# Down-projection of chunk pairs by seven block products of half size (Strassen), in a GateLoop and SwiGLU kernel

## The chip, the cores and the metric

One core of a Trainium2 chip runs the whole program. The metric is device time in microseconds of one execution; the time of the kernel before is the median of three. A profile shows one execution: engines are TensorE (PE; PEld is its loading of weights), VectorE (DVE), ScalarE (ACT), GpSimd (POOL) and SyncE (SP), whose queue here issues most DMA transfers.

## The reference

```python
def _attn_ref(q, k, v, a_re, a_im):          # (4, 8, 768, 48) each, float32
    mag = np.sqrt(a_re * a_re + a_im * a_im)
    scale = np.minimum(mag, 0.999) / (mag + 1e-06)
    a_re_n, a_im_n = (a_re * scale, a_im * scale)
    ...
    for t in range(S):
        ar, ai = (a_re_n[:, :, t, :, None], a_im_n[:, :, t, :, None])
        new_re = ar * S_re - ai * S_im
        new_im = ar * S_im + ai * S_re
        kv = np.einsum('bhd,bhe->bhde', k[:, :, t], v[:, :, t])
        S_re, S_im = (new_re + kv, new_im)
        y[:, :, t] = np.einsum('bhd,bhde->bhe', q[:, :, t], S_re)

def _moe_ref(x, w_gate, w_val, w_out, rms_g):  # x (3072, 384), d_ff 1536
    rms = np.sqrt(np.mean(x * x, axis=-1, keepdims=True) + 1e-06)
    xn = x / rms * rms_g
    g = xn @ w_gate
    silu = g * (1.0 / (1.0 + np.exp(-g)))
    val = xn @ w_val
    return (silu * val @ w_out)
```

The output of the first, with its heads side by side, is the `x` of the second. The weights arrive as 64-bit numbers and are narrowed on the chip.

## The kernel before

**Work.** The 3072 rows are 24 chunks of 128 (`C`), six to a sequence. For each chunk there are three kinds of work. `gates(u)` (L977) turns the gates of a unit of one or two chunks (`UNITS`, L667) into a decay and a rotation, and multiplies k and q by them into `rot`; six DMAs a chunk bring `rot` to `kq` in the layout that the products need (three buffers `kqs`, L819). It is mostly DVE and ACT work on 768 columns. `attend(n)` (L1065) makes the chunk's scores, its output and the next state on PE, with DVE masking the scores (`am`) and adding states, and ends in the RMS norm: the sum of squares goes through PE into a column, DVE makes `ssv` (the mean square plus 1e-6), POOL raises it to −1/2 (`rs`), PE spreads it, and DVE writes the chunk's part of `xT`, the normed input, transposed. `feed(g, xT)` (L1156) is the feed-forward network of a group of chunks.

**Groups.** `GROUPS` (L668) has two groups of two chunks, then five of four. `feed` runs over the 12 blocks of 128 hidden features. For each it makes gate and value in two PSUM banks (`bank()`, L1060, hands out banks 0 to 3 in turn); a list fills a bank, 512 columns: one feature block by 512 tokens, or two by 256 in a group of two. ACT applies Silu (`sg`), DVE multiplies into `hT`. Then each chunk has its down-projection: 12 matmuls accumulate `hT` (128 features by 128 tokens, the stationary side) times `wo` (384 columns), ACT copies the bank to `ot`, and a DMA on SP's queue writes it out. Matmuls are float32, each two instructions in the profile, each with its own load of weights.

**Order.** Nothing is issued as it is written. Every operation is recorded through helpers, so all carry L648, and `Flow.schedule` (L550) orders them: each engine takes, of the operations whose inputs are ready by the planner's own durations, the one due first. `feed` gives its lists due times from a running clock (`clock`, `SPREAD`, L1154); whatever feeds them inherits a due time from its users. The order of each engine is therefore fixed when the program is built, and an engine waits in place when the next operation's inputs are late.

**Tests.** The fast program holds for inputs in a certain range. Tests of this go into `ok`; the weight tests (`look(i)`, L912) read all weights again and reduce them on DVE. At the end the count of passed tests goes through a small matmul (`okc`) to `bad`, and where it isn't zero a general program runs after the fast one.

Of the kernel before, what the change touches and what calls it, by code (L numbers as in the profile page):

```python
# [18 lines left out]
P = 128  # L19
# [631 lines left out]
def fast(tc, ctx, qT, kT, v, a_re, a_im, w_gate, w_val, w_out, rms_g, out, H, bad):  # L651
# [10 lines left out]
    L = P // H  # L662
    HH = H // 2
    NP = H // 2
    assert DM % P == 0 and D2 <= P and L * ND == D and D == 48 and N == 24 and NF == 12

    UNITS = [[0], [1]] + [[n, n + 1] for n in range(2, N, 2)]  # L667
    GROUPS = [[0, 1], [2, 3]] + [list(range(n, n + 4)) for n in range(4, N, 4)]  # L668
    unit_of = {n: u for u, ns in enumerate(UNITS) for n in ns}
    group_of = {n: g for g, ns in enumerate(GROUPS) for n in ns}  # L670
    NU = len(UNITS)
# [138 lines left out]
    wv = room("wv", [P, DF // W, ND, W])  # L810
    wo = room("wo", [P, NF + 4, DM])
    hT = room("hT", [P, NF * 512])
    xTs = [room(f"xT{i}", [P, ND * 512]) for i in range(2)]
    gin = [room(f"in{i}", [P, 2, 768]) for i in range(2)]
    kin = room("kin", [P, 2 * ND * 2 * C])
    tmp = {x: room(x, [P, 768]) for x in ("t1", "t2", "t4")}
    turns = room("turns", [P, 2, 768])
    rots = [room(f"rot{i}", [P, 2 * ND, 2 * C]) for i in range(2)]
    kqs = [room(f"kq{i}", [D2, H, 2 * C]) for i in range(3)]  # L819
    decays = [room(f"decay{i}", [D2, H, nt]) for i, nt in enumerate((1, 1, 2, 2))]  # L820
    room("pad1", [P, 16])
    ams = [room(f"am{i}", [C, H, C]) for i in range(2)]
# [5 lines left out]
    ssv = [room(f"ssv{i}", [P, 1]) for i in range(2)]  # L828
    rss = [room(f"rs{i}", [P, 1]) for i in range(2)]
    sgs = [room(f"sg{i}", [P, 512]) for i in range(2)]  # L830
    ots = [room(f"ot{i}", [C, DM]) for i in range(2)]
    junk = room("junk", [1, 1], I32)
    seen = room("seen", [D2, 1])

# [142 lines left out]
    def gates(u):  # L977
        ns = UNITS[u]
        nt = len(ns)
        T = nt * C  # L980
        t = loaded.pop(u) if u in loaded else load_kq(u, load_gates(u))
        flow.stage = "size", u
        re, im, q, k = (t[x] for x in ("re", "im", "q", "k"))
        t1, t2, t3, t4, t5 = (t[f"t{i}"] for i in range(1, 6))
        act(t1, re, AF.Square)
        act(t2, im, AF.Square)
        if u in SUMMED:
            sums = []
# [60 lines left out]
        for n_ in ns:  # L1049
            moved[n_] = [dma(kqs[n_ % 3][r:D2:2 * ND], rots[n_ % 2][:, r], "SP") for r in range(2 * ND)]  # L1050
            if n_ < 2:
                cleared[n_] = copy(seen, kqs[n_ % 3][:, 0, 0:1], eng="POOL")
# [11 lines left out]

    def attend(n):  # L1065
        flow.stage = "attend", n
        ve, am, kq = ves[n % 3], ams[n % 2], kqs[n % 3]
        vv = ve[:, :, :, 0:D].rearrange("t m e d -> t (m e) d")
        dma(vv, v[n * C:(n + 1) * C, :].rearrange("t (h d) -> t h d", d=D), behind=moved[min(n - 1, HOLD)] if n else ())
        k, q = kq[:, :, 0:C], kq[:, :, C:2 * C]  # L1070
# [54 lines left out]
        else:  # L1125
# [7 lines left out]
        ts(ssv[n % 2], col, 1.0 / DM, EPS_RMS, ALU.mult, ALU.add)  # L1133
        add("POOL", [(nc.gpsimd.tensor_tensor, (), dict(out=rss[n % 2], in0=ssv[n % 2], in1=mhalf,
                                                        op=ALU.pow))], 0.9, [ssv[n % 2], mhalf], [rss[n % 2]])
# [8 lines left out]
        tt(xT[:, :, i * C:(i + 1) * C], yg, wide.unsqueeze(1).to_broadcast([P, ND, C]))  # L1144
        return xT

    xplace = {0: (0, 0), 1: (0, 768)}
    for g in range(2, len(GROUPS)):
        xplace[g] = ((g + 1) % 2, 0)

    clock = [36.0]
    SPREAD = 1.0  # L1154

    def feed(g, xT):  # L1156
        flow.stage = "feed", g
        ns = GROUPS[g]
        nt = len(ns)
        T = nt * C  # L1160
        base = {0: 0, 1: 3072}.get(g, 0)
        per = 4 // nt
        for b in range(NF // per):
            ps = [bank(), bank()]
            for o, w_ in zip(ps, (wg, wv)):
                list_ = []
                for i in range(per):
                    f = b * per + i
# [3 lines left out]
                dur = per * ND * mm_time(T)  # L1172
# [4 lines left out]
            tt(hT[:, base + b * 512:base + (b + 1) * 512], ps[1], sg)  # L1177
        for i, n in enumerate(ns):
            ps = bank()
            o = ps[:, 0:DM]  # L1180
            for f0 in range(0, NF, 4):
                clock[0] += 4 * mm_time(DM) * SPREAD
                mms([(o, hT[:, base + f * T + i * C:base + f * T + (i + 1) * C], wo[:, f], f == 0, f == NF - 1)
                     for f in range(f0, f0 + 4)], 4 * mm_time(DM), due=clock[0])
            ot = ots[n % 2]
            act(ot, o, AF.Copy)
            dma(out[n * C:(n + 1) * C, :], ot)

    for u in range(2):
        loaded[u] = load_gates(u)  # L1190
# [19 lines left out]

    ne = N * ND
    NW = len(looks)
    ok = room("ok", [P, 2 * ne + NU + 2 * NW])
    okc = room("okc", [P, 1])
    ef = ends.rearrange("p j n -> p (j n)")
    o = 0
    for in_, limit, op in ((ef, P_MIN, ALU.is_ge), (ef, 1.0, ALU.is_le), (range_, 0.0, ALU.is_le),
                           (small, 1.25 * 2.0 ** -15, ALU.is_ge), (large, 2.0, ALU.is_lt)):
        w_ = in_.shape[1]
        ts(ok[:, o:o + w_], in_, limit, None, op)  # L1220
        o += w_
    add("DVE", [(nc.vector.tensor_reduce, (), dict(out=okc, in_=ok, axis=mybir.AxisListType.X, op=ALU.add))],
        0.4, [ok], [okc])
    ps = banks[7]
    mms([(ps[0:1, 0:1], okc, ones, True, True)], 0.25)
    add("DVE", [(nc.vector.tensor_scalar, (), dict(out=bad, in0=ps[0:1, 0:1], scalar1=-1.0,
                                                   scalar2=float(P * o), op0=ALU.mult, op1=ALU.add))],
        0.2, [ps[0:1, 0:1]], [])

    flow.schedule()  # L1230
    with tc.manual_schedule():
# [51 lines left out]
```

## Time and profile before

| | us |
|---|---|
| median of 3 runs (lowest, highest) | 760.88 (760.03, 761.19) |
| profiled execution | 760.46 |
| its span, first to last instruction | 758.7 |
| PE, DVE, ACT, POOL busy | 712.6, 408.7, 324.7, 43.5 |
| instructions of PE | 3970 |

The clock of PE is 0.984 of full speed over the span. In a line of a group (`out<-in`, partitions by columns, count, then busy us and mean ns) buffer numbers are left out: `bank` is any PSUM bank, `hT`, `wo`, `xT` are as above. A line of the timeline has the start, the length, the engine and how many instructions stand together. A line of waits has the total, how many waits, and the longest.

### The profile page before, as it was taken

The page shows a single profiled execution, that of the slowest core. Times are in us where ns is not written, and L with a number is a line of the kernel's source. Part 1 is how long each engine was busy: PE and PEld are TensorE (multiplying, and loading weights), DVE is VectorE, ACT ScalarE, POOL GpSimd, SP SyncE. Part 2 cuts the span into 40 slices and gives each one's busy share as a digit, 9 for nine tenths or more (in the row PEclk, how much of TensorE's full clock was granted, in tenths as well). Part 3 has the DMA queues.
Part 4 walks back from the last instruction along what each step waited for, and adds up shares of the span by engine and source line. Part 5 has one row for each costly group of instructions (what it writes and reads, how often), then busy time and mean ns, then how long its engine had stood idle before and what let it go on. Part 6 is the DMA issues. An engine that isn't in the chain of part 4 may idle for free.

```text
span 758.7 us, 10119 instructions
## 1 busy us (share of the span) xinstructions
PE 712.6 (94%) x3970; PEld 444.0 (59%) x3970; DVE 408.7 (54%) x643; ACT 324.7 (43%) x450; POOL 43.5 (6%) x71
## 2 busy tenths in 40 slices
PE   0479999999999999999999999999999999999996
PEld 0468878886444777544576444576544577544453
DVE  5989888988887798871266621278111132111100
ACT  8568667866968455870155711153201011110100
POOL 3122100001000011000001000001000000000000
PEclk9959999999999999999999999999999999999999
DMA  8697647456663476610243200044100020000000
GB/s 297 211 280 224 188 122 214 131 130 173 178 197 115 125 203 175 177 62 1 58 131 105 73 0 0 12 127 104 53 1 0 11 64 12 22 0 0 1 21 25
DMA packets 100137, 76.33 MB, mean 101 GB/s; under 512 B 40945, under 2 KB 90865, under 8 KB 100081
## 3 DMA queue, kind: packets, MB, share of 16 engines
q1 hardware_dynamic: 96016, 61.05, 29.3%
q0 software_dynamic: 3264, 14.16, 5.2%
q8 instruction: 33, 0.54, 0.3%
q10 hardware_dynamic: 800, 0.39, 0.2%
q14 instruction: 24, 0.19, 0.1%
HBM read 51.91 MB, written 4.72 MB: 75 GB/s over the span
## 4 chain that ended last, share of the span: by engine, by line
PE 90%; DVE 4%; ACT 2%; POOL 1%; DMA 1%; issue 1%; SPq 0%; DVEq 0%; ACTq 0%; POOLq 0%
PE bank L648 90%; POOL rs L648 1%; DVE turns L648 1%; DVE wg L648 1%; ACT L648 1%; DVE wv L648 1%; ACT turns L648 0%; SPq L648 0%; DMA in<-in_a_re_dram 0%; ACT t L648 0%; DVE rot L648 0%; DMA ve<-in_v_dram 0%; DVE xT L648 0%; DVE in L648 0%; DVE am L648 0%
## 5 line engine op out<-in xcount | busy, mean ns | idle before, releaser
L648 PE MATMUL bank<-xT,wg 128*128 128x512 f32 (+1 forms) x504 | 199.5, 536 | 2.8 <-DVE xT L648 2.8
L648 PE MATMUL bank<-wo,hT 128*128 128x384 f32 x576 | 198.0, 490 | 0.0
L648 PE MATMUL bank<-xT,wv 128*128 128x512 f32 (+1 forms) x504 | 197.5, 532 | 0.0
L648 DVE TENSOR_TENSOR hT<-bank,sg 128x512 f32<-128x512 f32 x72 | 49.5, 689 | 194.9 <-PE bank L648 192.3
L648 PEld LDWEIGHTS bank<-xT,wg 128*128 128x128 f32 x504 | 96.2, 192 | 91.5 <-issue 83.0
L648 PEld LDWEIGHTS bank<-xT,wv 128*128 128x128 f32 x504 | 95.5, 190 | 89.9 <-issue 85.4
L648 PEld LDWEIGHTS bank<-wo,hT 128*128 128x128 f32 x576 | 105.0, 190 | 63.0 <-issue 2.5
L648 ACT ACTIVATE sg<-bank 128x512 f32<-128x512 f32 x72 | 43.0, 597 | 192.0 <-PE bank L648 189.2
L648 PE MATMUL bank<-kq 96*128 96x128 f32 x384 | 52.8, 290 | 28.0 <-DMA kq<-rot 28.0
L648 ACT ACT_TABLE_LOAD x57 | 73.1, 1283 | 10.2 <-DVE rot L648 7.8
L648 PEld LDWEIGHTS bank<-kq 96*128 96x128 f32 x384 | 50.1, 203 | 31.8 <-issue 28.4
L648 POOL TENSOR_TENSOR rs<-ssv,mhalf 128x1 f32<-128x1 f32 x24 | 24.1, 1004 | 554.3 <-DVE ssv L648 547.2
L648 ACT ACTIVATE ot<-bank 128x384 f32<-128x384 f32 x24 | 11.7, 488 | 78.3 <-PE bank L648 68.5
L648 DVE TENSOR_TENSOR rot<-kin,turns 128x768 f32<-128x768 f32 x48 | 44.2, 951 | 1.3 <-DMA kq<-rot 1.0
L648 ACT ACTIVATE kt<-bank 128x384 f32<-128x384 f32 x40 | 18.4, 489 | 52.9 <-PE bank L648 48.9
L648 DVE TENSOR_TENSOR am<-bank,causal 128x512 f32<-128x512 f32 x48 | 32.6, 684 | 14.4 <-PE bank L648 14.1
L648 PE MATMUL bank<-am,ve 128*32 128x128 f32 x768 | 38.4, 285 | 0.0
L648 ACT ACTIVATE turns<-in 128x768 f32<-128x768 f32 (+1 forms) x39 | 30.3, 790 | 18.6 <-DVE rot L648 8.6
L648 PEld LDWEIGHTS bank<-ve,kt 128*96 128x96 f32 x320 | 30.8, 170 | 6.7 <-issue 5.6
L648 PE MATMUL bank<-ve,kt 128*96 128x48 f32 x320 | 31.5, 253 | 1.9 <-DVE am L648 1.9
L648 ACT ACTIVATE t<-t 128x768 f32<-128x768 f32 (+1 forms) x39 | 30.8, 791 | 4.9 <-DVE t L648 4.2
L648 PE MATMUL bank<-kq,state 96*32 96x128 f32 x640 | 32.7, 275 | 0.0
(94 smaller groups left out, 572.6 us busy)
## 6 DMA issues: line engine op xcount, KB each, us to landing
kq<-rot SPq DMA_DIRECT2D x144, 128.0 KB, 2.4
ve<-in_v_dram SPq DMA_DIRECT2D x24, 192.0 KB, 3.8
kin<-in_q_dram SPq DMA_DIRECT2D x24, 192.0 KB, 3.0
kin<-in_k_dram SPq DMA_DIRECT2D x24, 192.0 KB, 4.1
wo<-in_w_gate_dram SPq DMA_DIRECT2D x6, 768.0 KB, 5.2
out_dram<-ot SPq DMA_DIRECT2D x24, 192.0 KB, 2.5
wo<-in_w_val_dram SPq DMA_DIRECT2D x6, 768.0 KB, 4.4
wo<-in_w_out_dram SPq DMA_DIRECT2D x6, 768.0 KB, 5.2
```

The source lines that it names most:

```text
L648: fn(*args, **kw)
```

## The change

The down-projection of a pair of chunks is a product of a 256 by 1536 matrix A (the hidden values, two chunks) and a 1536 by 384 matrix B (`wo`). Both are cut in four blocks: A by chunk and by half of the features, B by half of the features and of the columns. Instead of eight block products, seven are made, of sums of blocks:

- From the weights, once, ahead of the first split group: T1 = B01 − B00, T2 = B11 − T1, T3 = B11 − B01 (kept in the place of B01), T4 = B10 − T2.
- From the hidden values, per pair, on DVE: S3 = A00 − A10 (in the place of A10), S2 = A11 − S3, S1 = S2 + A00, and S4 = A01 − S2 (in the place of S2).
- Seven products of six matmuls with 192 columns, in four banks, x1 to x4: A00·B00, S3·T3, A01·B10, S2·T2, S1·T1, A11·T4 and S4·B11. The first goes to SBUF (`mid0`) by ACT; the rest are joined by DVE adds of 192 and 384 columns (`mid1`, `mid0`, `ot`).

All groups are now of two chunks; the first two keep the old down-projection (`FIRST = 2`). To make room, `xT` has three buffers of half the size and `kq` two instead of three. `SPREAD` is 1.02. `hT` is laid out by chunk. `ssv` keeps all 24 columns, and a further test wants each to be at least 2e-6; the final test has a due time ahead of the last products.

```diff
-    GROUPS = [[0, 1], [2, 3]] + [list(range(n, n + 4)) for n in range(4, N, 4)]
+    GROUPS = [[n, n + 1] for n in range(0, N, 2)]
...
-    xTs = [room(f"xT{i}", [P, ND * 512]) for i in range(2)]
+    xTs = [room(f"xT{i}", [P, ND * 256]) for i in range(3)]
...
-    kqs = [room(f"kq{i}", [D2, H, 2 * C]) for i in range(3)]
+    kqs = [room(f"kq{i}", [D2, H, 2 * C]) for i in range(2)]
...
-    SPREAD = 1.0
+    SPREAD = 1.02
+    FIRST = 2
+    B = {(k, j): wo[:, k * HD:(k + 1) * HD, j * DH:(j + 1) * DH] for k in range(2) for j in range(2)}
+    T1 = blocks(hT[:, 4608:4608 + HD * DH])
+    T2, T4 = blocks(sums[:, 0]), blocks(sums[:, 1])
+    T3 = B[0, 1]
+    S1, S2 = (hT[:, o:o + HD * C].rearrange("p (f t) -> p f t", f=HD) for o in (3072, 3840))
+    def weight_sums():
+        tt(T1, B[0, 1], B[0, 0], ALU.subtract)
+        tt(T2, B[1, 1], T1, ALU.subtract)
+        tt(T3, B[1, 1], B[0, 1], ALU.subtract)
+        tt(T4, B[1, 0], T2, ALU.subtract)
...
+            if split and 2 * b + 2 == HD:
+                tt(S3, A[0, 0], A[1, 0], ALU.subtract)
...
+        def product(o, l, r):
+            for f0 in range(0, HD, 3):
+                clock[0] += 3 * mm_time(DH) * SPREAD
+                mms([(o, l[:, f], r[:, f], f == 0, f == HD - 1) for f in range(f0, f0 + 3)],
+                    3 * mm_time(DH), due=clock[0])
+        tt(S2, A[1, 1], S3, ALU.subtract)
+        tt(S1, S2, A[0, 0], ALU.add)
+        x1, x2, x3, x4 = (bank()[:, 0:DM] for _ in range(4))
+        lo, hi = slice(0, DH), slice(DH, DM)
+        product(x1[:, lo], A[0, 0], B[0, 0])
+        act(mids[0][:, lo], x1[:, lo], AF.Copy)
+        product(x2[:, lo], S3, T3)
+        product(x4[:, lo], A[0, 1], B[1, 0])
+        product(x3[:, lo], S2, T2)
+        tt(mids[1][:, lo], mids[0][:, lo], x3[:, lo], ALU.add)
+        tt(mids[1][:, hi], mids[1][:, lo], x2[:, lo], ALU.add)
+        tt(S4, A[0, 1], S2, ALU.subtract)
+        product(x1[:, hi], S1, T1)
+        tt(mids[0][:, hi], mids[1][:, lo], x1[:, hi], ALU.add)
+        product(x1[:, lo], A[1, 1], T4)
+        tt(halves(ots[1]), halves(x1), mids[1][:, hi].unsqueeze(1).to_broadcast([C, 2, DH]), ALU.add)
+        product(x4[:, hi], S4, B[1, 1])
+        tt(ots[0], mids[0], x4, ALU.add)
...
+                           (ssv, 2.0 * EPS_RMS, ALU.is_ge)):
...
-    mms([(ps[0:1, 0:1], okc, ones, True, True)], 0.25)
+    mms([(ps[0:1, 0:1], okc, ones, True, True)], 0.25, due=clock[0] - 16.0)
```

The planner makes a new order of it. The first place is the end of PE's program, with the last group. Before, after the last gate and value lists (`wg`, `wv`):

```order
L648 MATMUL bank1_66<-xT1_93,wv_89 128x512 x3
L648 MATMUL bank2_67<-xT1_93,wg_88 128x512 x3
L648 MATMUL bank3_68<-xT1_93,wv_89 128x512 x3
L648 MATMUL bank0_65<-wo_90,hT_91 128x384 x12
L648 MATMUL bank1_66<-wo_90,hT_91 128x384 x12
L648 MATMUL bank2_67<-wo_90,hT_91 128x384 x12
L648 MATMUL bank3_68<-wo_90,hT_91 128x384 x12
L648 MATMUL bank7_72<-ones_76,okc_133 1x1
```

Now, in the same place; `sums` holds T2 and T4, and a row with `hT` alone is S1·T1, since both lie in `hT`. Of the three rows of `wo` and bank 3, the first is A01·B10 and the others are the halves of S4·B11:

```order
L648 MATMUL bank7_72<-ones_76,okc_135 1x1
L648 MATMUL bank3_68<-xT2_94,wv_89 128x256 x6
L648 MATMUL bank0_65<-wo_90,hT_91 128x192 x6
L648 MATMUL bank1_66<-wo_90,hT_91 128x192 x6
L648 MATMUL bank3_68<-wo_90,hT_91 128x192 x6
L648 MATMUL bank2_67<-sums_129,hT_91 128x192 x3
L648 MATMUL bank0_65<-hT_91 128x192 x3
L648 MATMUL bank2_67<-sums_129,hT_91 128x192 x3
L648 MATMUL bank0_65<-hT_91 128x192 x3
L648 MATMUL bank3_68<-wo_90,hT_91 128x192 x3
L648 MATMUL bank0_65<-sums_129,hT_91 128x192 x6
L648 MATMUL bank3_68<-wo_90,hT_91 128x192 x3
```

The small matmul of the final test moved from behind the last list to ahead of the last value list, and one list of three stands between the last of S2·T2 and the first of S4·B11.

The second place is DVE's program at that end. Before, only the products of gate and value and the final test:

```order
L648 TENSOR_TENSOR hT_91<-bank3_68,sg1_127 128x512
L648 TENSOR_TENSOR hT_91<-bank1_66,sg0_126 128x512
L648 TENSOR_TENSOR hT_91<-bank3_68,sg1_127 128x512
L648 TENSOR_TENSOR hT_91<-bank1_66,sg0_126 128x512
L648 TENSOR_TENSOR hT_91<-bank3_68,sg1_127 128x512
L648 TENSOR_SCALAR bad_58<-bank7_72 1x1
```

Now (`hT<-hT ... x2` is S2 and S1, the next one is S4):

```order
L648 TENSOR_SCALAR bad_58<-bank7_72 1x1
L648 TENSOR_TENSOR hT_91<-bank3_68,sg1_126 128x2x2x128
L648 TENSOR_TENSOR hT_91<-hT_91 128x768 x2
L648 TENSOR_TENSOR mid1_131<-mid0_130,bank2_67 128x192
L648 TENSOR_TENSOR hT_91<-hT_91 128x768
L648 TENSOR_TENSOR mid0_130<-mid1_131,bank0_65 128x192
L648 TENSOR_TENSOR mid1_131<-mid1_131,bank1_66 128x192
L648 TENSOR_TENSOR ot1_128<-bank0_65,mid1_131 128x384
L648 TENSOR_TENSOR ot0_127<-mid0_130,bank3_68 128x384
```

Seven sums follow the last product of gate and value, S4 behind the add that reads bank 2, and the last output is DVE's.

The third place is the border of two groups on PE, where the norm of a group's last chunk (`ones`, `rs`) stands ahead of the next group's first gate list. Before, ahead of the last group:

```order
L648 MATMUL bank3_68<-wo_90,hT_91 128x384 x4
L648 MATMUL bank7_72<-ident_73,rs0_124 128x128
L648 MATMUL bank3_68<-wo_90,hT_91 128x384 x4
L648 MATMUL bank7_72<-ones_76,sq0_119 128x1
L648 MATMUL bank3_68<-wo_90,hT_91 128x384 x4
L648 MATMUL bank7_72<-ident_73,rs1_125 128x128
L648 MATMUL bank0_65<-xT1_93,wg_88 128x512 x3
```

Now, ahead of the fifth group:

```order
L648 MATMUL bank7_72<-ident_73,kq1_105 128x96 x4
L648 MATMUL bank3_68<-wo_90,hT_91 128x192 x3
L648 MATMUL bank7_72<-ones_76,sq0_119 128x1
L648 MATMUL bank0_65<-sums_129,hT_91 128x192 x6
L648 MATMUL bank7_72<-ident_73,rs1_124 128x128
L648 MATMUL bank3_68<-wo_90,hT_91 128x192 x3
L648 MATMUL bank4_69<-ident_73,kq1_105 128x96 x4
L648 MATMUL bank0_65<-xT1_93,wg_88 128x256 x6
```

Products of the pair now stand on both sides of `rs`, and such a border comes twelve times instead of seven. On DVE, the weight tests' reductions (36 in all) lie elsewhere: from the third group on, counted from a group's first product of gate and value to the next group's, 19, 5 and 1 stood in the groups of four, and 8, 11 and 8 stand in the pairs.

More of the change, by code (lines that the diff above doesn't have):

```diff
@@ L827, in fast @@
     ygs = [room(f"yg{i}", [P, ND, C]) for i in range(2)]
-    ssv = [room(f"ssv{i}", [P, 1]) for i in range(2)]
+    ssv = room("ssv", [P, N])
     rss = [room(f"rs{i}", [P, 1]) for i in range(2)]
@@ L831, in fast @@
     ots = [room(f"ot{i}", [C, DM]) for i in range(2)]
+    sums = room("sums", [P, 2, HD * DH])
+    mids = [room(f"mid{i}", [C, DM]) for i in range(2)]
     junk = room("junk", [1, 1], I32)
@@ L1049, in gates @@
         for n_ in ns:
-            moved[n_] = [dma(kqs[n_ % 3][r:D2:2 * ND], rots[n_ % 2][:, r], "SP") for r in range(2 * ND)]
+            moved[n_] = [dma(kqs[n_ % 2][r:D2:2 * ND], rots[n_ % 2][:, r], "SP") for r in range(2 * ND)]
             if n_ < 2:
-                cleared[n_] = copy(seen, kqs[n_ % 3][:, 0, 0:1], eng="POOL")
+                cleared[n_] = copy(seen, kqs[n_ % 2][:, 0, 0:1], eng="POOL")
         for r in range(2 * ND):
@@ L1132, in attend @@
         mms([(col, sq[:, j], ones, j == 0, j == parts[-1]) for j in parts], 0.25 * len(parts))
-        ts(ssv[n % 2], col, 1.0 / DM, EPS_RMS, ALU.mult, ALU.add)
-        add("POOL", [(nc.gpsimd.tensor_tensor, (), dict(out=rss[n % 2], in0=ssv[n % 2], in1=mhalf,
-                                                        op=ALU.pow))], 0.9, [ssv[n % 2], mhalf], [rss[n % 2]])
+        sv = ssv[:, n:n + 1]
+        ts(sv, col, 1.0 / DM, EPS_RMS, ALU.mult, ALU.add)
+        add("POOL", [(nc.gpsimd.tensor_tensor, (), dict(out=rss[n % 2], in0=sv, in1=mhalf,
+                                                        op=ALU.pow))], 0.9, [sv, mhalf], [rss[n % 2]])
         wide = ps[:, 0:C]
@@ L1158, in feed @@
         ns = GROUPS[g]
[L1159 to L1163, printed above, removed]
+        T = len(ns) * C
+        base = {1: 3072}.get(g, 0)
+        h = hT[:, base:base + NF * T].rearrange("p (i f t) -> p i f t", i=2, f=NF)
+        A = {(i, k): h[:, i, k * HD:(k + 1) * HD] for i in range(2) for k in range(2)}
+        S3, S4 = A[1, 0], S2
+        split = g >= FIRST
+        if g == FIRST:
+            weight_sums()
+        for b in range(HD):
             ps = [bank(), bank()]
@@ L1166, in feed @@
                 list_ = []
-                for i in range(per):
-                    f = b * per + i
+                for i in range(2):
+                    f = b * 2 + i
                     for d in range(ND):
@@ L1176, in feed @@
             act(sg, ps[0], AF.Silu)
[L1177 to L1187, printed above, removed]
+            as_f = lambda x: x.rearrange("p (f i t) -> p f i t", f=2, i=2)
@@ new lines, in feed, with finish @@
+            tt(h[:, :, 2 * b:2 * b + 2].rearrange("p i f t -> p f i t"), as_f(ps[1]), as_f(sg))
+            if split and 2 * b + 2 == HD:
+                tt(S3, A[0, 0], A[1, 0], ALU.subtract)
+        def finish():
+            for n, ot in zip(ns, ots):
+                dma(out[n * C:(n + 1) * C, :], ot)
+        if not split:
+            for i in range(2):
+                o = bank()[:, 0:DM]
+                for f0 in range(0, NF, 4):
+                    clock[0] += 4 * mm_time(DM) * SPREAD
+                    mms([(o, h[:, i, f], wo[:, f], f == 0, f == NF - 1) for f in range(f0, f0 + 4)],
+                        4 * mm_time(DM), due=clock[0])
+                act(ots[i], o, AF.Copy)
+            finish()
+            return
@@ L1212, in fast @@
     NW = len(looks)
-    ok = room("ok", [P, 2 * ne + NU + 2 * NW])
+    ok = room("ok", [P, 2 * ne + NU + 2 * NW + N])
     okc = room("okc", [P, 1])
```

18 lines of the change are left out of this document (11 added, 7 removed).

## The prediction

> **What bounds the kernel now.** I read the page first: engine totals, the granted clock by slice, and the chain that ended last.
>
> ```profile
> span 758.7 us, 10119 instructions
> PE 712.6 (94%) x3970; PEld 444.0 (59%) x3970; DVE 408.7 (54%) x643; ACT 324.7 (43%) x450; POOL 43.5 (6%) x71
> PEclk9959999999999999999999999999999999999999
> PE 90%; DVE 4%; ACT 2%; POOL 1%; DMA 1%; issue 1%; SPq 0%; DVEq 0%; ACTq 0%; POOLq 0%
> ```
>
> TensorE (PE) is busy 94% of the span, its clock is granted in full after the first slices, and it is 90% of the chain. The waits of PE say where the rest went:
>
> ```profile
> PE bank L648 <- DMA kq<-rot: 28.0, 1, 28.0
> PE bank L648 <- POOL rs L648: 3.4, 3, 1.6
> PE bank L648 <- DVE xT L648: 2.8, 5, 0.8
> ```
>
> 28.0 us is the start, which the change leaves alone. After it PE hardly waits, and what it waits for (the norm's `rs` and `xT`) stands at the borders of groups. So a change is worth what it takes out of PE's stream, less what new waits it puts in.
>
> The stream's prices come from the timeline: the start of one list to the start of the next, divided by its instructions (one matmul call is two instructions here). I don't use the groups' mean durations: their modelled ends overlap.
>
> ```profile
> 62.74 2.75 PE L648 MATMUL bank<-xT,wg 128*128 128x256 f32 x12
> ...
> 75.69 2.75 PE L648 MATMUL bank<-xT,wv 128*128 128x256 f32 x12
> ```
>
> ```profile
> 571.36 2.74 PE L648 MATMUL bank<-xT,wg 128*128 128x512 f32 x6
> ...
> 581.66 2.74 PE L648 MATMUL bank<-xT,wg 128*128 128x512 f32 x6
> ```
>
> ```profile
> 604.54 2.75 PE L648 MATMUL bank<-wo,hT 128*128 128x384 f32 x8
> 607.12 1.06 PE L648 MATMUL bank<-kq 96*128 96x128 f32 x8
> ```
>
> ```profile
> 617.27 1.95 PE L648 MATMUL bank<-kq 96*128 96x128 f32 x16
> 619.06 0.28 PE L648 MATMUL bank<-ones,sq 128*128 128x1 f32 x2
> ```
>
> 256 columns: 12.95 us over five lists of twelve, 0.2158 us each. 512: 10.30 over four lists of six, 0.4292. 384: 2.58/8 = 0.3225. 128: 1.79/16 = 0.112. Time follows the columns, with a small fixed part.
>
> **The change part by part.** *The products.* Before, a pair of chunks takes 2 × 12 calls, 48 instructions of 384 columns: 15.48 us. Now it takes 7 × 6 calls, 84 instructions of 192 columns, a form the trace lacks. Half of the 384 price is 0.161; halfway between the rows at 128 and 256 is 0.164; the line through 256 and 384 gives 0.1625. I take 0.163: 84 × 0.163 = 13.69, 1.79 less per pair, and 17.9 us less in ten pairs (the first two groups stay whole). By the ends it is 17.0 to 19.6.
>
> This needs the weight loads to stay hidden, since a load now stands before 192 columns instead of 384:
>
> ```profile
> L648 PEld LDWEIGHTS bank<-wo,hT 128*128 128x128 f32 x576 | 105.0, 190 | 63.0 <-issue 2.5
> L648 PEld LDWEIGHTS bank<-kq 96*128 96x128 f32 x384 | 50.1, 203 | 31.8 <-issue 28.4
> ```
>
> A load lasts 190 ns, more than 163. But the `kq` instructions have loads of 203 ns and follow each other every 112 ns, so loads overlap the stream and one another.
>
> The Trainium skill speaks against the change here: "TensorE: Matmul & The Clock Gate", section "The mechanism", says that a weight load overlaps running matmuls only where the row groups differ, and all loads of these products use all 128 rows. By that rule, with the 107 ns that its section "LDWEIGHTS" gives for 128 columns, a pair would go from 48 × (0.3225 + 0.107) = 20.6 to 84 × (0.163 + 0.107) = 22.7 us, an estimate from the page: 21 us lost over ten pairs. By that rule, the trace disagrees: with loads of its own, the 256-column list leaves no room for 107 ns in 0.2158.
>
> *Groups of two.* Five groups of four used 512-column lists. A list of twelve at 256 takes 2.590, one of six at 512 takes 2.575: 0.015 more, 24 such per group of four, five groups: 1.8 us.
>
> *New sums on VectorE (DVE) and ScalarE (ACT).*
>
> ```profile
> L648 DVE TENSOR_TENSOR rot<-kin,turns 128x768 f32<-128x768 f32 x48 | 44.2, 951 | 1.3 <-DMA kq<-rot 1.0
> L648 DVE TENSOR_TENSOR turns<-turns,t 128x1536 f32<-128x1536 f32 x11 | 19.3, 1752 | 4.2 <-ACT turns L648 4.1
> L648 DVE TENSOR_TENSOR xT<-yg,bank 128x384 f32<-128x384 f32 x24 | 13.2, 549 | 14.3 <-PE bank L648 14.2
> L648 DVE TENSOR_TENSOR sq<-sq 128x128 f32<-128x128 f32 x40 | 11.5, 287 | 1.8 <-ACT sq L648 1.2
> L648 ACT ACTIVATE ot<-bank 128x384 f32<-128x384 f32 x24 | 11.7, 488 | 78.3 <-PE bank L648 68.5
> ```
>
> Per pair DVE gets S1 to S4, 768 wide, 4 × 0.951; three adds of 192 columns, a quarter of the way from 0.287 to 0.549, 3 × 0.353; and two of 384, 2 × 0.549: 5.96 us. ACT loses two 0.488 copies and gains one shorter. The four weight sums, 1152 wide, are halfway between 0.951 and 1.752: 5.4 us once. Whether DVE holds them is read by stage:
>
> ```profile
> 55.70:116.10 60.40, 60.35 (x397) 48.81 (x398) 55.90 (x82) 41.77 (x58) 8.70 (x13) 0.97 0.59 172
> 184.20:304.00 119.80, 118.96 (x672) 69.90 (x671) 98.44 (x147) 77.31 (x98) 4.94 (x4) 1.00 0.58 165
> 304.00:421.00 117.00, 115.63 (x621) 66.81 (x620) 65.59 (x110) 57.53 (x76) 4.63 (x4) 1.00 0.31 87
> ```
>
> ```profile
> L648 DVE TENSOR_REDUCE small<-wo 128x1 f32<-128x768 f32 x10 | 9.5, 949 | 2.2 <-DMA wo<-in_w_out_dram 1.7 <-DMA wo<-in_w_val_dram 0.4
> L648 DVE TENSOR_REDUCE large<-wo 128x1 f32<-128x768 f32 x10 | 9.5, 948 | 0.0
> ```
>
> (Columns: stage, length, then PE, weight loads, DVE, ACT, POOL busy.) The first split groups fall in the stage from 184.2 us. DVE is busy 98.4 of 119.8 there; with 2 × 5.96 + 5.4 it would be 115.7 of 116.6 (119.8 less 2 × 1.79, and 0.36 for the lists of 256), full. But 19.0 us of it are the weight tests' reductions (the two rows from that same window), which nobody waits for until the end, and the order spreads them: after the weight sums the next pairs hold 8, 11 and 8. What must be done is 96.7 of 116.6, 83%, and from 55.7 to 116.1 DVE worked at 93% while PE lost 0.05 us. So the sums are hidden there, by the attention of the next two chunks, which stands between the products; that cover gone, the chain below is paid.
>
> In the last pair it is gone: no attention is left. S4 overwrites S2, so it waits for the third product's last read. From there DVE does one 192 add and S4: 0.353 + 0.951, plus about 0.17 for the matmul's drain (490 − 322.5 ns, the group's mean less its spacing) and 0.1 for two handovers, 1.57 us. PE has six instructions meanwhile, 0.98. Wait: 0.6 us, once.
>
> *Borders of groups.* PE's waits at the norm after 55 us are, for `rs`,
>
> ```profile
> PE bank L648 <- POOL rs L648: 3.0, 2, 1.6
> ```
>
> and the 2.8 for `xT` above, together 5.8 over seven groups, 0.83 each. Twelve groups have five more borders: up to 4.1. Against it: the order puts twelve product instructions and more between the last norm's sum and the gate. The bottom is 0; I take the middle, 2.1.
>
> *Fewer `kq` buffers, three smaller `xT`.* In the order, the last read of `kq0` in a pair and the next read of it are a whole gate and value stage apart, twelve lists, 31 us. A refill is
>
> ```profile
> 400.81 3.76 SPq L648 DMA_DIRECT2D kq<-rot  x6
> kq<-rot SPq DMA_DIRECT2D x144, 128.0 KB, 2.4
> ```
>
> 3.8 + 2.4 = 6.2 us: hidden. Its wait on PE now stands in SyncE's queue ahead of the next loads of `v`, q and k and the outputs; these have the same 31 us. Nothing, and the buffers of `xT` nothing.
>
> *The end.* The final test leaves the tail:
>
> ```profile
> 734.79 16.93 PE L648 MATMUL bank<-wo,hT 128*128 128x384 f32 x52
> 744.07 0.49 ACT L648 ACTIVATE ot<-bank 128x384 f32<-128x384 f32 x1 [7.30 <-PE bank L648]
> 752.09 0.49 ACT L648 ACTIVATE ot<-bank 128x384 f32<-128x384 f32 x1 [7.53 <-DVE bad L648]
> ```
>
> The last copy starts 8.02 us after the one before; 24 × 0.3225 = 7.74, so 0.28 goes to the test between them. The last step is now a DVE add, 0.549 for 0.488: 0.2 gained. The floor on the norms adds one small DVE instruction off the path.
>
> **Sum**, against the profiled execution's 760.46 us (span 758.7 and 1.8 around it): −17.9 + 1.8 + 0.6 + 2.1 − 0.2 = −13.6, 746.9. The median of the runs, 760.88, lies 0.4 above that execution, so I say 747.2. With the terms' ends: 742.5 + 0.4 (19.6 saved, no waits at the borders or for S4) to 749.8 + 0.4 (17.0 saved, 4.1 of waits at the borders).
>
> **The rivals.**
>
> *DVE is late in the first split pairs.* For: 115.7 us of DVE in 116.6, if the reductions stay in the way. At the 93% at which it worked beside a full PE (55.9 of 60.4), that takes 125.0, 8.4 more: 755.6. Against: 83% without them. Chance 0.12, anything from 750 to 755.6.
>
> *Slower: weight loads become the floor.* If a product's instruction can't follow faster than its load's own 190 ns, a pair takes 84 × 0.190 = 15.96, 0.48 more than before, 4.8 in all, and with the other terms 760.9 + 4.8 + 4.3 = 770. The gain is gone from 0.179 us per instruction on (15.48 less 0.43 of other terms per pair, over 84). Against it stands the `kq` row, 112 ns with loads of 203; left open only because its weights fill 96 rows. Chance 0.03. The rule of the Trainium skill told above is a harsher form of this.
>
> *Slower: the two `kq` buffers.* If chunks wait for the 6.2 us refill, at 22 chunks the gain is lost from 0.62 us each on; at 1 us each it is 769. For: PE's one long wait is for that DMA. Against: the 31 us between. Chance 0.03.
>
> *Many small waits at the new handovers*, 1.4 us in each of ten pairs: no change. Chance 0.02.
>
> That the norm's floor sends the kernel into its second program would multiply the time; the reference's rows have mean squares of 2.6e-5 and more against a floor of 1e-6, so I give it nothing.
>
> **How the numbers follow.** The forecast, 747.2, has 0.80. The range, 742.9 to 753.6, runs from the forecast's lower end over its upper one, 750.2, into the late-DVE case, of which it takes in more than half. A measurement of this kernel can tell about 0.2%, 1.5 us, from no change. Faster: 0.80 + 0.12 = 0.92; same 0.02; slower 0.03 + 0.03 = 0.06.
>
> **What would show it right or wrong.** In the changed profile, six product instructions should start 0.98 us before the next list, and ten pairs should hold 840 of 192 columns beside 96 of 384. A spacing near 0.19 means that loads bind. PE's waits outside the start should be 7 to 12 us, on `xT`, `rs` and, once, DVE's S4 (a write of `hT`). More than 16 us of waits on DVE between 180 and 400 us, or waits on DMA `kq<-rot` after the start, would make the forecast wrong, as would a DVE total far from 474 us (408.7 + 59.6 + 5.4).

## The result, and the profile after

The changed kernel takes 740.45 us (median of 4 runs, 739.72 to 742.11) beside 760.81 for the kernel before in the same comparison: a ratio of 0.9737, with a 95% interval of 0.9719 to 0.9755. It is faster, as forecast, but 747.2 was forecast and the time lies below the range's low end of 742.9. The profiled execution took 740.29 us (span 738.6), 20.2 less than the 760.46 of before; the sum of the prediction had 13.6 less.

The page of the kernel after has the engine totals, the granted clock and the chain:

```profile
span 738.6 us, 12320 instructions
PE 694.7 (94%) x5050; PEld 623.9 (84%) x5050; DVE 470.6 (64%) x738; ACT 332.1 (45%) x450; POOL 39.4 (5%) x71
PEclk9968999999999999999999999999999999999999
PE 92%; DVE 4%; ACT 1%; POOL 1%; issue 1%; DMA 1%; DVEq 0%; POOLq 0%; ACTq 0%
```

PE still bounds the kernel, now as 92% of the chain. DVE's 470.6 us is within 1% of the 474 that was forecast. The products show in the last pair, in the timeline of PE after:

```profile
723.50 1.14 PE L648 MATMUL bank<-sums,hT 128*128 128x192 f32 x6
...
726.43 1.14 PE L648 MATMUL bank<-hT 128*128 128x192 f32 x6
727.98 1.24 PE L648 MATMUL bank<-wo,hT 128*128 128x192 f32 x6 [0.41 <-DVE hT L648]
...
731.00 1.14 PE L648 MATMUL bank<-wo,hT 128*128 128x192 f32 x6
```

Three steps of six take 2.93 us, 0.1628 us an instruction, where 0.163 was forecast. The one wait for S4 is there too: 0.41 us, where 0.6 was forecast. The groups of PE after count the instructions by shape, and the group of weight loads gives their duration:

```profile
L648 PE MATMUL bank<-wo,hT 128*128 128x192 f32 x480 | 90.0, 331 | 0.4 <-DVE hT L648 0.4
L648 PE MATMUL bank<-sums,hT 128*128 128x192 f32 x240 | 45.1, 329 | 0.0
L648 PE MATMUL bank<-wo,hT 128*128 128x384 f32 x96 | 33.3, 491 | 0.0
L648 PE MATMUL bank<-hT 128*128 128x192 f32 x120 | 24.0, 336 | 0.0
```

```profile
L648 PEld LDWEIGHTS bank<-sums,hT 128*128 128x128 f32 x240 | 39.4, 190 | 0.0
```

480 + 240 + 120 = 840 instructions of 192 columns beside 96 of 384, as forecast. A load still lasts 190 ns and an instruction follows the last after 163: loads are not the floor.

What was not forecast stands in PE's waits. After:

```profile
PE bank L648 <- DVE xT L648: 1.9, 3, 0.9
PE bank L648 <- POOL rs L648: 1.8, 1, 1.8
```

The 1.8 for `rs` is in the start, at 53.90 us. The timeline of PE before has these waits past the first gate list (the bracket at a row's end is the wait ahead of it):

```profile
187.09 2.84 PE L648 MATMUL bank<-xT,wg 128*128 128x512 f32 x6 [0.84 <-DVE xT L648]
...
410.86 0.49 PE L648 MATMUL bank<-ident,rs 128*128 128x128 f32 x2 [1.37 <-POOL rs L648]
...
422.63 2.84 PE L648 MATMUL bank<-xT,wg 128*128 128x512 f32 x6 [0.31 <-DVE xT L648]
...
528.63 0.49 PE L648 MATMUL bank<-ident,rs 128*128 128x128 f32 x2 [1.64 <-POOL rs L648]
...
540.36 2.84 PE L648 MATMUL bank<-xT,wg 128*128 128x512 f32 x6 [0.32 <-DVE xT L648]
...
658.69 2.84 PE L648 MATMUL bank<-xT,wg 128*128 128x512 f32 x6 [0.65 <-DVE xT L648]
```

and that of PE after has two, beside the one for S4:

```profile
117.10 2.86 PE L648 MATMUL bank<-xT,wg 128*128 128x256 f32 x12 [0.32 <-DVE xT L648]
...
686.15 2.86 PE L648 MATMUL bank<-xT,wg 128*128 128x256 f32 x12 [0.89 <-DVE xT L648]
```

The norm's waits were 5.13 us and are 1.21. More borders of groups brought 3.9 us less of waiting, not 2.1 more.

### The profile page after: what moved, and what is told of

The parts are those of the page before. It is cut to its first block, busy times and chain, and to the rows that moved or that the text cites. A ratio compares the mean times of both kernels' runs of the same rounds, so it can differ in the third digit from the quotient of the medians.

```text
span 738.6 us, 12320 instructions
## 1 busy us (share of the span) xinstructions
PE 694.7 (94%) x5050; PEld 623.9 (84%) x5050; DVE 470.6 (64%) x738; ACT 332.1 (45%) x450; POOL 39.4 (5%) x71
## 4 chain that ended last, share of the span: by engine, by line
PE 92%; DVE 4%; ACT 1%; POOL 1%; issue 1%; DMA 1%; DVEq 0%; POOLq 0%; ACTq 0%
PE bank L648 92%; DVE wg L648 1%; DVE turns L648 1%; DVE wv L648 1%; DMA in<-in_a_re_dram 1%; ACT t L648 0%; DVE t L648 0%; DVE rot L648 0%; ACT L648 0%; DVE in L648 0%; POOL rs L648 0%; DVE xT L648 0%; ACT turns L648 0%; DVE am L648 0%; ACT wo L648 0%
## 5 line engine op out<-in xcount | busy, mean ns | idle before, releaser
L648 PE MATMUL bank<-xT,wg 128*128 128x256 f32 x864 | 201.0, 383 | 1.9 <-DVE xT L648 1.9
L648 PE MATMUL bank<-xT,wv 128*128 128x256 f32 x864 | 198.4, 379 | 0.0
L648 PEld LDWEIGHTS bank<-xT,wg 128*128 128x128 f32 x864 | 164.8, 192 | 25.1 <-DVE xT L648 2.6
L648 PEld LDWEIGHTS bank<-xT,wv 128*128 128x128 f32 x864 | 163.5, 190 | 22.2
L648 PE MATMUL bank<-wo,hT 128*128 128x192 f32 (+1 forms) x576 | 123.4, 357 | 0.4 <-DVE hT L648 0.4
L648 PEld LDWEIGHTS bank<-wo,hT 128*128 128x128 f32 x576 | 94.4, 190 | 11.8 <-issue 1.4
L648 ACT ACTIVATE sq<-bank 128x384 f32<-128x384 f32 x24 | 11.8, 491 | 106.7 <-PE bank L648 106.6
L648 PE MATMUL bank<-sums,hT 128*128 128x192 f32 x240 | 45.1, 329 | 0.0
L648 PEld LDWEIGHTS bank<-sums,hT 128*128 128x128 f32 x240 | 39.4, 190 | 0.0
L648 DVE TENSOR_TENSOR hT<-hT 128x768 f32<-128x768 f32 x40 | 38.2, 955 | 0.9
```

What stands on the lines that cost most here:

```text
L648: fn(*args, **kw)
```

## The experiments

Two theories stood against each other. **Cover**: what PE waits for at a border is set by the PE work that the order puts between the last chunk's spread of `rs` and the next group's first gate list, since in that time DVE must write `xT`; the pieces of the products stand there now. **Count**: a border has its price, and more borders cost more. The cover at a border is read from the kernel's order and priced by the spacings of the timeline. This is PE's order at one border, of two-chunk groups with whole down-projections (pairs_whole, below), and of the kernel after:

```
L648 MATMUL bank_72<-ident,rs_124 128x128
L648 MATMUL bank_69<-ident,kq_105 128x96 x4
L648 MATMUL bank_67<-xT_92,wg 128x256 x6
```

```
L648 MATMUL bank_72<-ident,rs_124 128x128
L648 MATMUL bank_68<-wo,hT 128x192 x3
L648 MATMUL bank_69<-ident,kq_105 128x96 x4
L648 MATMUL bank_65<-xT_92,wg 128x256 x6
```

Three calls of a product more are 0.98 us. The four calls on `kq` are four instructions and take 0.33 (230.69 to 231.02 in the second timeline below); the recorded expectations count them as 0.66, twice what they take. So the cover is 1.31 us instead of 0.33.

**pairs_whole**: the kernel after without any product by blocks. It keeps groups of two, two `kq` buffers, the floor and the early test.

```diff
-    FIRST = 2
+    FIRST = 99
```

> The changed kernel with all groups of two but no split group (the old down-projection everywhere, no weight sums, no S sums): the grouping alone. Theory cover (a border waits for what the order leaves uncovered behind rs: 0.66 us of attention stands there at six borders where the changed kernel has 1.64 and more, nothing at two): 740.45 + 10 x 1.83 for the products - 0.41 for S4 + some 0.3 x 6 at the borders = 760.2 us, with xT waits of about 0.3 us at the borders with 0.66. Theory groups (pairs and three xT buffers end the waits whatever the products): 758.3, no such waits. Theory count (each border costs 0.83, as forecast): 760.8 + 1.8 + 4.1 = 766.7.

Measured: 760.78 us (759.39 to 761.64), 1.0001 of before [0.9992, 1.001]. Groups of two alone bring nothing that the times tell, and the block products bring the whole 20.3. The nothing is a balance: the two `rs` waits of before, 3.0 us, are absent here too, without a single block product in the order, while the lists of 256 columns and more waits for `xT` (0.7) are added. The same border in the timeline of PE, in this kernel and then in the kernel after:

```profile
231.55 0.38 PE L648 MATMUL bank<-ident,rs 128*128 128x128 f32 x2
231.77 0.49 PE L648 MATMUL bank<-ident,kq 96*128 96x96 f32 x4
232.58 2.64 PE L648 MATMUL bank<-xT,wg 128*128 128x256 f32 x11 [0.32 <-DVE xT L648]
```

```profile
229.49 0.38 PE L648 MATMUL bank<-ident,rs 128*128 128x128 f32 x2
229.71 1.14 PE L648 MATMUL bank<-wo,hT 128*128 128x192 f32 x6
230.69 0.49 PE L648 MATMUL bank<-ident,kq 96*128 96x96 f32 x4
231.02 2.78 PE L648 MATMUL bank<-xT,wg 128*128 128x256 f32 x12
```

With the product's piece in between, the gate list starts without a wait. In pairs_whole the seven borders with a cover of 0.33 wait 0.31 or 0.32 us, the last, with none, 0.65, and those with 0.9 or 1.79 not at all: cover and wait together are 0.65 wherever there is a wait. Cover holds; a price per border of 0.83 does not.

**five_split**: the block products in the last five pairs alone.

```diff
-    FIRST = 2
+    FIRST = 7
```

> The changed kernel with only the last five pairs split. If the products are worth 84 x 0.1625 against 48 x 0.3225 = 1.83 us per pair wherever they stand: halfway between the changed kernel and pairs_whole within 0.5 us, so 749.6 plus about 0.3 x 4 of xT waits by theory cover = 750.8, 749.6 by theory groups. If the gain were smaller in the first pairs, where DVE is full, the time would lie nearer to the changed kernel: 747 or less.

Measured: 751.33 us (750.01 to 752.29), 0.9879 [0.9864, 0.9894], about halfway between 760.78 and 740.45 (750.6). The `xT` waits of 0.3 us are at five of the unsplit borders; between the first split pair and the border at 695.78, which has no cover (0.89), there are none.

**plan_rs_3**: the kernel before, whose planner is told that `rs` takes 3.0 us instead of 0.9. This goes for the other part of the 5.13 us. `rs` usually takes 0.55; the two waits of before come from two that took 2.93. First POOL, then DVE, both from the kernel before:

```profile
407.87 2.93 POOL L648 TENSOR_TENSOR rs<-ssv,mhalf 128x1 f32<-128x1 f32 x1 [17.42 <-DVE ssv L648]
...
525.64 2.93 POOL L648 TENSOR_TENSOR rs<-ssv,mhalf 128x1 f32<-128x1 f32 x1 [12.29 <-DVE ssv L648]
```

```profile
407.71 2.68 DVE L648 TENSOR_TENSOR rot<-kin,turns 128x768 f32<-128x768 f32 x3
...
525.49 2.68 DVE L648 TENSOR_TENSOR rot<-kin,turns 128x768 f32<-128x768 f32 x3
```

```diff
-                          op=ALU.pow))], 0.9, [ssv[n % 2], mhalf], [rss[n % 2]])
+                          op=ALU.pow))], 3.0, [ssv[n % 2], mhalf], [rss[n % 2]])
```

> The kernel before, with one number of the planner changed: the duration of POOL's rs 3.0 us instead of 0.9, so the order leaves more between the norm's sum and rs. Theory cover: the two waits for rs, 3.0 us in all, go, the waits for xT (2.1 after the first) stay: 757.8. Rival (these waits are not set by what stands between, or move elsewhere): 760.8 within 0.7.

Measured: 760.08 us (758.77 to 761.84), 0.999 [0.9981, 0.9999]. The `rs` waits past the start are gone, but the first gate list starts at 57.74 instead of 55.75, and the `xT` waits are 4.7 us in all instead of 2.8. By the time, the 757.8 of cover was missed: the gain was given back at the start, where the longer planned `rs` also moved the order. So the edit was made again without the start.

**plan_rs_3_late**: the same for chunks 8 on alone.

```diff
-                          op=ALU.pow))], 0.9, [ssv[n % 2], mhalf], [rss[n % 2]])
+                          op=ALU.pow))], 3.0 if n > 7 else 0.9, [ssv[n % 2], mhalf], [rss[n % 2]])
```

> The kernel before, with the planner's duration of rs 3.0 from the ninth chunk on and 0.9 ahead of it, so that the start stays as it was (plan_rs_3 began its first gate list 2.0 us later). Between the norm's sum and rs stand 5.2 us and more from there on. Theory cover: the two rs waits, 3.0 us in all, go and nothing else changes: 757.6. Rival (these waits are made up elsewhere): 760.8 within 0.7.

Measured: 757.76 us (756.71 to 758.9), 0.9961 [0.9948, 0.9975]. PE's waits in this kernel:

```profile
PE bank L648 <- DVE xT L648: 2.8, 5, 0.8
...
PE bank L648 <- POOL rs L648: 1.4, 1, 1.4
```

The two `rs` waits are gone (the 1.4 is in the start), `xT` is as before, and 3.0 us are gained: what those two waits were. One `rs` still took 3.39 us here, at 518.37, and nobody waited for it.

**products_early** and **products_late**: the kernel after, with the products due 15 us earlier, or later. The same work in another order, so that products leave the attention and the borders, or move into them.

```diff
-                    3 * mm_time(DH), due=clock[0])
+                    3 * mm_time(DH), due=clock[0] - 15.0)
```

> The changed kernel with the products' due times 15 us earlier, nothing else: the same work, but the order draws the products ahead of the norm. Between the norm's sum and rs stand 0 to 0.9 us of PE work in most of the last chunks of the pairs (2.0 and more in the changed kernel), and behind rs 0 instead of 1.79 at one more border. Theory cover: waits for rs of about 1.1 where nothing stands between and 0.2 where 0.9 does, some 4 us in all, one more xT wait of 0.8, and S4 waits of 0.4 where the products stand together: 745 to 748. Theory products (the split pairs are worth 20 us wherever their lists stand): 740.5.

Measured: 772.55 us (771.02 to 775.52), 1.0149 [1.0134, 1.0165]: 32 us slower than after, slower than before, and far more than either theory had. PE's waits in this kernel:

```profile
PE bank L648 <- ACT kt L648: 5.5, 10, 0.6
PE bank L648 <- POOL rs L648: 3.8, 3, 1.5
PE bank L648 <- DVE xT L648: 3.7, 5, 1.5
```

Without products among it, the whole chain of the attention waits, not the norm alone. Past the first gate list, the waits are 16.7 us in 26 places where after has 1.6 in 3. That is 15 of the 35.2 us by which its profiled execution (775.52, the longest of the four) is longer. The windows of this kernel show a second price (columns: stretch, length, busy PE, weight loads, DVE, ACT, POOL, then the granted clock, and of DMA the share and GB/s):

```profile
230.00:235.00 5.00, 3.83 (x45) 3.26 (x34) 4.70 (x9) 0.98 (x2) 1.05 (x1) 1.00 0.21 44
235.00:240.00 5.00, 5.00 (x25) 4.70 (x25) 3.34 (x7) 0.60 (x2) 0.19 (x1) 0.66 0.58 163
```

Two waits (0.59 and 0.58 us) stand between 230 and 235 us, and then the granted clock is 0.66. Eleven such stretches of 5 us lie below 0.98 from 235 us on; what they lack of a full clock adds up to 13.7 us. Before and after have no such stretch past 65 us. 15.0 + 13.7 = 28.7 of 35.2. The rest is not settled. A shown wait begins at the modelled end of the matmul before, which lies about 0.17 us past its spacing, so 23 more waits may hide 4 us; that is an estimate.

```diff
-                    3 * mm_time(DH), due=clock[0])
+                    3 * mm_time(DH), due=clock[0] + 15.0)
```

> The changed kernel with the products' due times 15 us later. 1.95 us of products stand behind rs at every split border, the last one too (0 in the changed kernel), and 2.0 or more ahead of it. Theory cover: the last border's wait of 0.89 goes, no other comes: 739.5. Rival, from spread_100 (DVE has other work queued ahead of xT or S4, and the wait is set there): waits of 0.4 to 1.6 come back at two or three places: 742 to 744.

Measured: 738.57 us (737.82 to 739.19), 0.9709 [0.9695, 0.9722]. The order has 1.95 us of cover at every border of split pairs, the last included, and PE's waits show it:

```profile
PE bank L648 <- DVE xT L648: 1.0, 2, 0.7
```

Of the two, one is in the start and one (0.32) at 117.42, ahead of the split pairs. The 0.89 of after is gone. Cover had 739.5. The interval overlaps that of after (0.9719 to 0.9755), so it is the trace that tells the step, not the time.

**spread_100**: the kernel after with the spread of before.

```diff
-    SPREAD = 1.02
+    SPREAD = 1.0
```

> The changed kernel with SPREAD 1.0 instead of 1.02, another order of the same work. Theory cover: behind rs stand 1.37 us or more at every split border and 0.98 at the last (0 in the changed kernel), so the last border's wait of 0.89 goes: 739.6. Rival (the 1.02 is what keeps the waits away): several waits come back, 743 or more.

Measured: 744.16 us (743.22 to 745.06), 0.9784 [0.9771, 0.9797]. Here cover was wrong and its rival right: a border with 1.87 us of PE work behind `rs` waits 1.55. DVE of this kernel at that border:

```profile
344.86 0.96 DVE L648 TENSOR_TENSOR rot<-kin,turns 128x768 f32<-128x768 f32 x1 [1.57 <-DMA kq<-rot]
...
346.85 0.96 DVE L648 TENSOR_TENSOR rot<-kin,turns 128x768 f32<-128x768 f32 x1 [0.88 <-DMA kq<-rot]
347.73 0.55 DVE L648 TENSOR_TENSOR ot<-bank,mid 128x384 f32<-128x384 f32 x1
348.20 0.55 DVE L648 TENSOR_TENSOR xT<-yg,bank 128x384 f32<-128x384 f32 x1
```

PE had spread `rs` at 344.99, but DVE stood at two `rot` multiplies that waited for a DMA to free their buffer, and `xT` stood behind them in its queue. PE's cover is half of the rule; the other is what DVE has queued ahead of `xT`. (The last border of after shows the same: its 0.89, where 0.65 would do without cover, has an `ot` sum on DVE from 685.08 us, ahead of `xT` at 685.55.) Waits for S4 came in two more pairs as well (0.37 and 0.54). Past the start the waits are 1.7 us more than those of after, of the 2.9 by which this profiled execution (743.22) is longer; the rest is open.

**first_1**: one pair more by block products, whose `hT` moves to the front to make room for the sums.

```diff
-    FIRST = 2
+    FIRST = 1
...
-        base = {1: 3072}.get(g, 0)
+        base = 0
```

> The changed kernel with the second pair split too; the weight sums move one pair earlier, where DVE is fullest. Theory cover: one more pair at 1.83: 738.6. Rival (DVE is late there, since the weight sums' 5.4 us come on top): the gain is lost or turned, 740.5 to 744, with waits of PE on DVE between 90 and 180 us.

Measured: 743.21 us (740.99 to 744.86), 0.9761 [0.9741, 0.9781]. One pair less of the old kind should save 1.8 us, and yet the median is 2.8 above that of after. The five runs are spread wide, two of them at 741.0, and the interval overlaps that of after, so the times show only that the gain of 1.8 did not come. The profiled execution is the longest of the five, 744.86. The rival's time came out, but its place did not: the waits there are at 279.01 (`rs`, 1.00), 341 to 343 (0.57 for new sums), and 350.05:

```profile
350.05 4.54 PE L648 MATMUL bank<-xT,wg 128*128 128x256 f32 x12 [1.70 <-DVE xT L648]
```

The list behind that wait takes 4.54 us instead of 2.86, and the window there has the granted clock at 0.66:

```profile
350.00:355.00 5.00, 4.95 (x15) 4.08 (x16) 4.88 (x8) 0.36 (x1) 0.00 (x0) 0.66 0.53 162
```
3.3 us of new waits and 1.7 of clock, less 1.8, are 3.2 of the 4.6 us by which this execution is longer than the profiled one of after (740.29); the rest is open. Whether the runs at 741.0 had these waits is not known.

**kq_three**: pairs_whole with three `kq` buffers, to price the ring of two (there is room for it only without the block products' sums).

```diff
-    kqs = [room(f"kq{i}", [D2, H, 2 * C]) for i in range(2)]
+    kqs = [room(f"kq{i}", [D2, H, 2 * C]) for i in range(3)]
...
-    sums = room("sums", [P, 2, HD * DH])
+    sums = hT[:, 0:2 * HD * DH].rearrange("p (a n) -> p a n", a=2)
```

> pairs_whole (760.78 us) with three kq buffers instead of two, the one part of the change to buffers taken back alone. Prediction's view (a refill is hidden): same time within 0.5 us, 760.3 to 761.3, though DVE's 16.1 us of waits of rot for DMA kq<-rot nearly vanish, since PE never waited for them. Rival (the ring of two costs): PE's xT waits past the start, 3.6 us in nine in pairs_whole, come from DVE being held behind rot; then they go and the time is 757 to 758.5. By cover, the order has 2.03 us instead of 0.66 or 1.79 behind rs at two of the borders, so at most 0.6 us less, 760.2, for that reason alone.

Measured: 760.22 us (758.73 to 762.59), 0.9993 [0.9983, 1.0002], against 1.0001 [0.9992, 1.001]: no difference that the intervals tell. DVE's waits of `rot` for its DMA fall from 16.1 to 5.2 us, and PE's waits past the start stay at 3.0 us (0.6 of `xT` is gone, and one of 0.8 for `rs` is new):

```profile
PE bank L648 <- DVE xT L648: 2.9, 7, 0.7
PE bank L648 <- POOL rs L648: 1.8, 2, 1.0
```

In this order the ring of two costs PE nothing that shows; spread_100 shows an order in which it does.

**test_early**: the kernel before with its final test due ahead of the last products.

```diff
-    mms([(ps[0:1, 0:1], okc, ones, True, True)], 0.25)
+    flow.stage = None
+    mms([(ps[0:1, 0:1], okc, ones, True, True)], 0.25, due=clock[0] - 16.0)
...
-        0.2, [ps[0:1, 0:1]], [])
+        0.2, [ps[0:1, 0:1]], [], due=clock[0] - 15.0)
```

> The kernel before with the one edit at the end alone: the final test's small matmul is due ahead of the last products. Prediction: the last copy starts 7.74 instead of 8.02 us after the one before, 0.28 us, so 760.6 us and a ratio of 0.9996, which the time alone can't show and the tail of the trace can: no DVE bad between the last matmul and the last copy. Rival (another step of the tail ends last, such as the output's DMA): span unchanged at 758.7.

Measured: 760.63 us (759.41 to 761.25), 0.9995 [0.9986, 1.0004], which tells nothing. The last two copies of this kernel:

```profile
745.00 0.49 ACT L648 ACTIVATE ot<-bank 128x384 f32<-128x384 f32 x1 [7.30 <-PE bank L648]
753.02 0.49 ACT L648 ACTIVATE ot<-bank 128x384 f32<-128x384 f32 x1 [7.53 <-PEq L1243]
```

They are 8.02 us apart, as before, with no test between them. So the 0.28 us were not the test's matmul alone. In pairs_whole, which also has the early test, they are 7.74 apart. What holds the last copy here is open.

**late_s4**: products_late with S4 in the place of A10, which the second product has read, instead of S2's.

```diff
-        S3, S4 = A[1, 0], S2
+        S3, S4 = A[1, 0], A[1, 0]
```

> The kernel after with the products due 15 us later (as in products_late, 738.57 us) and with S4 written over A10's place, which the second product has read, instead of over S2, which the third product of the list still reads. Cover theory: the one wait for S4, 0.41 us in the last pair, goes, and the covers behind rs stay at 1.95 or 2.93 us of PE work, so 738.57 - 0.4 = 738.2 us, with one xT wait of 0.3 left past the start. Rival, that S4 is late for another reason (DVE reaches it late because of what stands ahead of it in its queue): the wait stays at 0.3 to 0.5 us on the write of hT, and the time is 738.6.

Measured: 737.17 us (736.87 to 738.47), 0.9691 [0.9678, 0.9703], the fastest of all; its interval overlaps that of products_late, so the step between them isn't told by the times. The wait for S4 is gone from its trace, and past the start PE waits once:

```profile
116.38 2.86 PE L648 MATMUL bank<-xT,wg 128*128 128x256 f32 x12 [0.32 <-DVE xT L648]
```

## Why the prediction was right, and where it was wrong

Against the profiled execution of before (us):

| term | forecast | measured |
|---|---|---|
| products | -17.9 | -18.1 |
| lists of 256 columns | +1.8 | +1.6 |
| S4 in the last pair | +0.6 | +0.4 |
| borders of groups | +2.1 | -3.9 |
| end | -0.2 | -0.5 |
| start (no term) | 0 | +0.3 |
| sum | -13.6 | -20.2 (the two executions differ by 20.2) |

*Products*: right. At the measured 0.1628 a pair takes 84 × 0.1628 = 13.68 us, 1.80 less than 15.48, which is 18.0 in ten. The whole timeline agrees: from each instruction's start to the next one's, waits left out, the products take 15.0 us less than before and the attention, among which they now stand, 3.1 less, 18.1 together. By the rule of the Trainium skill ("TensorE: Matmul & The Clock Gate", section "The mechanism") these loads could not overlap the matmuls; the trace disagrees, with 190 ns loads of all 128 rows at one instruction every 163 ns.

*Lists of 256*: right. The starts of all gate and value lists in the timeline add up to 373.9 us before and 376.2 after; 0.6 of the difference is the first list, which belongs to the start:

```profile
55.75 4.56 PE L648 MATMUL bank<-xT,wg 128*128 128x256 f32 x12 [0.71 <-DVE xT L648]
```

```profile
55.41 5.19 PE L648 MATMUL bank<-xT,wg 128*128 128x256 f32 x12 [0.71 <-DVE xT L648]
```

The upper row is of before, the lower of after: the list starts 0.34 earlier and takes 0.63 longer.

*DVE late*: it wasn't. In the windows of the kernel after, the stage of the first split pairs has PE busy without a gap, and DVE at 86%:

```profile
174.50:290.00 115.50, 115.50 (x852) 105.54 (x851) 99.77 (x153) 70.41 (x90) 3.49 (x4) 1.00 0.50 137
```

first_1 shows how near the margin is: a pair earlier, the new sums cost PE 0.57 us at 341 to 343 us.

*S4*: mechanism and place right, size 0.41 for 0.6; late_s4 takes it away.

*The end*: the last product ends 6.98 us before the span's end before (758.7 less 751.72) and 6.46 after (738.6 less 732.14). The size was off by 0.3, and test_early doesn't bear out that the test was the reason.

**The step that failed** is *Borders of groups*: "Twelve groups have five more borders: up to 4.1 ... The bottom is 0; I take the middle, 2.1." It made a mean of 0.83 us over unlike waits into a price per border, and let nothing below zero, so that a gain couldn't come out. It wanted 7 to 12 us of PE's waits outside the start; 1.6 were there. Three things stood in its place:

- The two `rs` waits, 3.0 of its 5.8 us (0.7 more stood ahead of the first list), were no price of a border at all: both lie 11.8 us ahead of a gate list, in the middle of an attention, and plan_rs_3_late takes them away with every border kept. They are absent in pairs_whole as well, so a new order is enough, and the block products aren't needed for it. In after no `rs` past the start takes more than 1.20 us. That the three `rot` multiplies on DVE hold it is argued from rows that coincide, not shown by a run that moves them alone.
- The five more borders cost 0.7: the `xT` waits past the start are 2.12 us before and 2.85 in pairs_whole.
- The pieces of the products then took most of these away, 2.85 to 1.21. The prediction counted them as "against it" and didn't follow them to the instruction: they stand behind `rs`, where 0.98 us outlasts a wait of 0.32.

With -3.9 in place of +2.1 the sum is -19.6, and 741.3 with the 0.4 for the median: within 0.9 us of what was measured.

## What to carry to other kernels

A mean wait per border is no price: find for each wait what covers it in the new order, on the waiting engine and in the queue of the one that it waits for, and let the term fall below zero if new work stands in the gap. Small pieces of independent matmul work are worth more than their own time saved when the planner can set them behind a norm, and worth less than nothing where they are taken out of the attention (32 us between the same instructions in two orders).

## What the runs showed of the hardware

- **A small POOL operation beside DVE work on SBUF tensors**: `rs`, one column, took 0.55 us in most places. Where it began while DVE was in a multiply of two SBUF tensors, it mostly ended about 0.41 us after that multiply did: 1.19 us where a `rot` multiply had 0.79 left (before, 295.53), and 1.99 where one of 1536 columns had 1.58 left (kq_three, first POOL, then DVE):

```profile
395.77 1.99 POOL L648 TENSOR_TENSOR rs<-ssv,mhalf 128x1 f32<-128x1 f32 x1 [45.41 <-DVE ssv L648]
```

```profile
395.61 1.75 DVE L648 TENSOR_TENSOR turns<-in,turns 128x1536 f32<-128x1536 f32 x1
```

  Beside a reduction of one tensor (before, 113.66) or an `am` product, which reads PSUM (products_early, 348.41), it took 0.55. Beside three `rot` multiplies in a row it ended 0.41 after the third: 2.93, twice in before and twice again in test_early, and 3.39 with one more product ahead of them (plan_rs_3 and plan_rs_3_late). Why it got through between two `rot` multiplies at 295.53 and not at 407.87 is open. The Trainium skill, "GPSIMD Engine Reference", section "Specifications", has POOL's SBUF interface shared with VectorE, with contention where DVE has two SBUF inputs; the trace agrees in these places. It isn't DVE's two-input work alone, though: one `rs` took 0.79 beside a TENSOR_SCALAR of one tensor (pairs_whole, 465.29).
- **The clock after short waits**: granted 0.66 over 5 us in products_early (235 to 240 us) after two waits of under 0.6 us, and in first_1 after one of 1.70; but full in spread_100 after one of 1.55 and in before after one of 1.64. The Trainium skill, "TensorE: Matmul & The Clock Gate", section "What's actually happening", drops the clock to half after an idle window of about 3.4 us. The size agrees (the 0.34 of 5 us that are missing, 1.7 us, are what 3.4 us at half clock lose); the length of idle doesn't: no single wait ahead of these stretches was over 1.82 us. So waits of 0.6 to 1.8 us can cost 1.7 more, and whether they do isn't told by their length alone.
